# Feature-axis DFT as one pair of 64-row tiles per cycle, sequence blocks of three or four cycles, and a rounding copy moved to ScalarE

## The chip, the cores and the metric

The kernel runs on one core of one Trainium2 chip. The metric is the device time of one execution in microseconds; the time before is the median of three runs, 2136.24 us (2133.95 to 2139.14). Engines are called as the profile calls them: PE (matmul), PEld (its weight loads), DVE (vector), ACT (scalar), POOL (GpSimd), SP (sync, which issues most DMAs here).

## The reference, cut to what matters

Two branches over one sequence of 2048 rows and 640 features are mixed by a gate per row.

```
g = sigmoid((x * gate_w).sum(-1))                       # x = A_x
qkv = x @ wqkv;  32 heads of 20;  p = softmax(q k^T / sqrt(20))
a = (p v) @ wo                                          # attention
re = x @ dft_hid_re^T;  im = x @ dft_hid_im^T           # DFT over the features
b = dft_seq_re @ re - dft_seq_im @ im                   # DFT over the sequence, real part
out = g * a + (1 - g) * b
```

Both branches read the same `A_x` (`xa` in the kernel).

## The kernel before

Every matmul that must be exact in float32 is made of three matmuls in a rounded format: a value is split into a rounded part and the rest (`split`, line 90: a rounding copy by one engine, a subtraction by another), and of the four products the three large ones are summed in PSUM.

A first part (up to about 255 us) makes the projections for queries, keys and values. Then comes the main loop (line 552) of 1024 steps: 16 pairs of heads, two halves of the queries for each (32 units), 16 key tiles, two query chunks. A step makes for each of the two heads of a pair one score matmul transposed (`mixed`, L573) whose exp goes to `p` on ACT (L576), and one score matmul for the unit that follows 41 steps later (`s_mm`, L150), whose maximum DVE takes (L152). A pair of such matmuls uses the two 64-row halves of the array. All of them take their PSUM banks in turn from the five of `bank`. Every fourth step, `av_step` (L402) multiplies the last four steps' exps by the values; these 16 matmuls are called the value block here, and four steps a cycle. At the end of a unit the sums are turned into reciprocals and sent through DRAM (`unit_end`, steps 1 to 21 behind it); the negated maxima of the next unit are written into rows of the queries by four small DMAs from SP (`max_chain`). At each new pair of heads (every 64 steps, every 16 cycles) POOL issues 16 DMAs that load the stacked keys and queries (L556).

The DFTs are put between the score matmuls. First the feature axis: 64 tiles (`hid_tile`: two halves of the features, real and imaginary part, 16 row tiles), each 15 matmuls over 128 rows into one of two banks `yp` in turn, one tile in each of the three steps of a cycle that hold no value block, and one in step 0. ACT copies the bank to `raw` with a sign (L282), and SP stores it. After 64 tiles (86 steps) the input and the weights are released and the buffers of the next stage are taken (`start_dft`).

Then the sequence axis, as seven products of a Strassen scheme (`PRODUCTS`): 7 x 8 units of 16 `dft_step`s, each of three pairs of 64-row matmuls (L476), the lower half of the rows into `yp[0]`, the upper into `yp[1]`. At a unit's end ACT copies one bank (L492) and DVE adds the other (L494), later adds the result into up to two outputs (`finish_y`). `goals` says how many pairs are done by which step; half of a step's pairs stand between its two `mixed`, half behind. Every unit takes four or five cycles. The DFT matrix of the sequence comes in blocks of eight steps: at the first step of a block (s % 8 == 0) `load_c` issues the loads for the block after the next (one or two of 512 KB, into `raw` and `raw2`), at s % 8 == 4 its `finish` adds the two on POOL (L373) and splits the result into a `part` on POOL (L94, L95). Three buffers each of `raw` and `part` turn round. `run_extras` runs due DVE work in the steps with a value block, and loads and splits the other operand, `araw` to `a`, on POOL, for the next product.

At the end the attention output is projected and the three parts are added.

Of the kernel before, what the change touches and what calls it, by code (L numbers as in the profile page):

```python
# [12 lines left out]
AF = mybir.ActivationFunctionType  # L13
ALU = mybir.AluOpType
# [4 lines left out]
P = 128  # L19
# [4 lines left out]
ND = D // P  # L24
NS = S // P
NP = H // 2
HE = D // 2
# [2 lines left out]
NU = 2 * NP  # L30
BW = HE + 2
LEAD = 41
DLAG = 5

# [10 lines left out]
HT = NS // 2  # L47
UNITS = len(PRODUCTS) * HT
# [7 lines left out]
def mix_kernel(ctx: ExitStack, tc: tile.TileContext, xa, wqk, wb, cdft, wo, out):  # L56
# [33 lines left out]
    def split(dst1, dst2, src, e1, e2):  # L90
        if e1 is act:
            act.activation(dst1, src, AF.Copy)  # L92
        else:
            e1.tensor_copy(dst1, src)  # L94
        e2.tensor_tensor(dst2, src, f32(dst1), op=ALU.subtract)  # L95
# [38 lines left out]
    now, later = [-1], {}  # L134

    def at_step(i, fn):
        later.setdefault(i, []).append(fn)
# [30 lines left out]
    yp = [None, None]  # L168

    def new_y(z):  # L170
        yp[z] = ps_y.tile([P, 512], F32, name=f"yp{z}")
        return yp[z]
# [65 lines left out]
    def flush(keep=0):  # L238
        while len(stores) > keep:
            sp.dma_start(*stores.pop(0))  # L240
# [12 lines left out]
    def mm_b(j, s, ps, n):  # L253
        w = wt["b", j]
        cs = slice(s * P, (s + 1) * P)
        for d in range(ND):
            three(ps[:, :n], xs[:, 0, d, cs], xs[:, 1, d, cs], w[:, 0, d, :n], w[:, 1, d, :n], d == 0, d == ND - 1)

    def v_pair(hf, s):
# [12 lines left out]
            vst.rearrange("p a k e -> p a (k e)")))  # L272
        flush(1)

    def hid_tile(i):
        j, st = divmod(i, NS)
        hf, ri = divmod(j, 2)
        g = -1.0 if ri else 1.0
        ps = new_y(i % 2)[:, :HE]
        mm_b(2 + j, st, ps, HE)  # L280
        a = raw_tile()[:, :HE]
        act.activation(a, ps, AF.Copy, scale=g)  # L282
        stores.append((a_scr[ri, hf, st], a))
        flush(1)

    step = 0

# [72 lines left out]
    def load_c(g):  # L360
        n, j = divmod(g, 2)
        n, t = divmod(n, HT)
        raws = []
        for i, (_, th, ri) in enumerate(PRODUCTS[n][0]):
            raw = apool[0].tile([P, 1024], F32, name="raw2", bufs=2) if i and apool else raw_tile()
            o = (2 * ri + j) * 1024
            sp.dma_start(raw, cdft[th * HT + t, :, o : o + 1024])
            raws.append(raw)

        def finish():  # L370
            c = cparts[g] = part_tile()
            if len(raws) > 1:
                pool.tensor_tensor(raws[0], raws[0], raws[1], op=ALU.add if PRODUCTS[n][0][1][0] > 0 else ALU.subtract)  # L373
            split(c[:, 0], c[:, 1], raws[0], pool, pool)

        return finish

# [29 lines left out]
    def unit_end(i, n):  # L407
# [36 lines left out]
        for k, fn in ((1, store_l), (4, load_l), (10, recip), (12, store_r), (15, load_r), (19, norm), (21, store_o)):  # L444
            if n == NU - 1:
                rest.append(fn)
            else:
                at_step(i + k, fn)

    wos = {}  # L450

    seen = set()
# [2 lines left out]
    def dft_step(g):  # L455
        n, t, s = g // NS // HT, g // NS % HT, g % NS
        if s == 0:
            new_y(0), new_y(1)
            outs[n, t] = []
            for _, th, hf in PRODUCTS[n][2]:  # L460
                y = apool[0].tile([P, HE], F32, name="yt", bufs=4)
                tt = th * HT + t
                if (tt, hf) in seen:
                    sp.dma_start(y, y_scr[tt, :, hf * HE : (hf + 1) * HE])
                outs[n, t].append(y)
        if s % 8 == 0 and g // 8 + 2 < 2 * UNITS:
            cfin.append(load_c(g // 8 + 2))
        if s % 8 == 4 and cfin:
            cfin.pop()()
        c = cparts[g // 8]  # L470
        cs = slice((s % 8) * P, (s % 8 + 1) * P)
        a = at[n % 2, s]
        for z, (cz, az) in enumerate(((0, 0), (0, 1), (1, 0))):
            for h in range(2):
                r = slice(64 * h, 64 * h + 64)
                pe.matmul(yp[h][:, :HE], c[r, cz, cs], a[r, az], start=s == 0 and z == 0, stop=s == NS - 1 and z == 2)  # L476
            if z < 2:
                yield
        w = g % (HT * NS) - 16
        if n + 1 == len(PRODUCTS) and w >= 0:  # L480
            d, r = divmod(w, 8)
            if r == 0 and d < ND:
                wos[d] = raw_tile()[:, :D]
                sp.dma_start(wos[d], wo[:, d])
            if r == 5 and d < ND:
                raw = wos.pop(d)
                for h in range(2):
                    wos[d, h] = a_tile(1, 2 * d + h)
                    split(wos[d, h][:, 0], wos[d, h][:, 1], raw[:, h * HE : (h + 1) * HE], pool, pool)
        if s == NS - 1:  # L490
            m = apool[0].tile([P, HE], F32, name="m", bufs=2)
            act.activation(m, yp[0][:, :HE], AF.Copy)  # L492
            y1 = yp[1][:, :HE]
            extras.append((now[0] + 1, lambda: dve.tensor_tensor(m, y1, m, op=ALU.add)))  # L494
            for out_, y in zip(PRODUCTS[n][2], outs.pop((n, t))):
                extras.append((now[0] + 2, functools.partial(finish_y, out_, t, m, y)))
        yield
# [32 lines left out]
    def start_dft():  # L530
        flush()
        proj.release()
        apool.append(pools(name="apool", bufs=1))
    HID = 4 * NS
    ops = {}

    def load_o(tt):
# [8 lines left out]
        return finish  # L546

    total = 32 * NU
    done = hid = hid_end = 0
    goals, fins = {}, {}  # L550
    dft = itertools.chain.from_iterable(dft_step(g) for g in range(NS * UNITS))
    for i in range(total + 1):
        now[0] = i
        n, s = divmod(i, 32)
        for fn in later.pop(i, ()):
            fn()  # L556
        if s % 2 == 0:
            flush()
        if i < total:
            kt, qc = divmod(s, 2)  # L560
            if s == 0 and n % 2 == 0:
                p = n // 2
                if p + 1 < NP:
                    at_step(i + 6, functools.partial(load_v, p + 1))
                    for j, args in enumerate(load_stack(p + 1)):
                        at_step(i + 2 + j // 2, functools.partial(pool.dma_start, *args))
            q, k = q_unit(n), kst[(n // 2) % 2]
            pp = pts[n, kt, qc] = pair_tile()

            def mixed(h):  # L570
                b = 64 * h
                pt = bank()
                pe.matmul(pt, k[b : b + KROWS + 2, kt * P : (kt + 1) * P],  # L573
                          q[b : b + KROWS + 2, qc * 512 : (qc + 1) * 512], start=True, stop=True)
                most = s_mm(i + LEAD, 1 - h)
                act.activation(pp[:, h], pt, AF.Exp, scale=float(DH) ** -0.5)  # L576
                most()

            mixed(0)
            half = (done + goals.get(i, done) + 1) // 2  # L580
            while done < half:
                next(dft)
                done += 1
            mixed(1)
            s_end(i + LEAD)
        if hid_end and hid_end + 2 <= i < hid_end + 2 + HT:
            for k in range(2):
                at_step(i + 3, load_a(0, 2 * (i - hid_end - 2) + k))
        if i and i % 4 == 0:
            j = i // 2 - 2  # L590
            for kt in (j, j + 1):
                av_step(i, kt // NS, kt % NS)
            run_extras(max(done - 1, 0) // 3, 2)
        elif not hid_end:
            if hid in (NS, 2 * NS):
                flush()
                load_wb(3 + hid // NS, pool, pool)()
            hid_tile(hid)
            hid += 1
            if hid in (4 * NS - 10, 4 * NS - 6):  # L600
                flush()
                load_c((hid - 4 * NS + 10) // 4)()
            if hid == 4 * NS:
                hid_end = i + 1
                start_dft()
        else:
            if not goals:

                first = -(-(hid_end + DLAG) // 4)
                fills = [j for j in range(4 * first, total - 4) if j % 4]  # L610
                edge = [u * (len(fills) // 3) // UNITS * 3 for u in range(UNITS + 1)]
                for u in range(UNITS):
                    for f in range(edge[u], edge[u + 1]):
                        goals[fills[f]] = 3 * NS * u + 3 * NS * (f - edge[u] + 1) // (edge[u + 1] - edge[u])
            while done < goals.get(i, 0):
                next(dft)
                done += 1
        if total - 10 <= i < total - 4 and i % 2 == 0:
            tt = (i - total + 10) // 2
            fins[tt] = load_o(tt)  # L620
        if i == total - 3:
            fins[0]()
    assert done == 3 * NS * UNITS
    now[0] = total + 4
    run_extras(2 * NS * UNITS, 99)
    for i in sorted(later):
# [69 lines left out]
```

## Time and profile before

| | us |
|---|---|
| median of three runs | 2136.24 |
| the profiled execution's own time | 2140.89 |
| its span in the profile | 2139.1 |
| PE busy | 2057.7 (96%) |
| DVE busy | 1474.3 (69%) |
| ACT busy | 1249.9 (58%) |
| POOL busy | 948.7 (44%) |

In the rows of the profile, a group names its line, engine, operation, the tile written and read, the shapes and the count; after the bar stand its busy time, the mean of one in ns, and the idle time of the engine just before it with what ended most of it. A row of the timeline gives the start, the length, the engine and line, the count of merged instructions, and in brackets the idle time before it and its releaser. A row by stretches gives the stretch, its length, then busy time and count by engine; its last three columns are the granted PE clock, the mean busy share of the DMA engines and GB/s.

### The profile page before, as it was taken

The numbers are of one execution on the slowest core, as the hardware profiler recorded it, in microseconds if no ns is written. First come the engines' busy times: TensorE is split into PE (matmuls) and PEld (weight loads), VectorE is DVE, ScalarE is ACT, GpSimd is POOL, SyncE is SP. The second block draws the span as 40 slices with busy tenths as digits, with TensorE's granted clock in tenths as the row PEclk, the third lists the DMA queues.
The fourth block names the chain that finished last, engine by engine and source line by source line (L and its number), as shares of the span: only waits on it lengthen the run. The fifth ranks groups of instructions, "written<-read, shape, count | busy, mean of one in ns | idle before, by whom it ended". The sixth has DMA issues, their size and how long they took to land. (4 is left out here: it accounts for less than half of the span.)

```text
span 2139.1 us, 41869 instructions
## 1 busy us (share of the span) xinstructions
PE 2057.7 (96%) x16120; PEld 1417.3 (66%) x16120; DVE 1474.3 (69%) x2452; ACT 1249.9 (58%) x2337; POOL 948.7 (44%) x834
## 2 busy tenths in 40 slices
PE   8999999999989999999998989998999899999999
PEld 7976667676656666666565656665666566666679
DVE  3055544446878787878787878887878688888623
ACT  4221244445657676767665766666767567777761
POOL 1100000115768244435694467536644477566420
PEclk9999999999999999999999999999999999999999
DMA  7663211134464334333745374525443645353345
GB/s 227 152 179 146 105 62 45 65 107 139 132 167 136 88 99 117 96 114 126 187 136 143 126 190 145 152 89 139 128 117 110 158 146 159 118 149 113 118 138 187
DMA packets 184216, 280.86 MB, mean 131 GB/s; under 512 B 63004, under 2 KB 127548, under 8 KB 180176
## 3 DMA queue, kind: packets, MB, share of 16 engines
q1 hardware_dynamic: 158992, 246.20, 37.4%
q0 software_dynamic: 25024, 31.99, 6.9%
q8 instruction: 126, 2.06, 0.4%
q14 instruction: 74, 0.61, 0.1%
HBM read 213.81 MB, written 63.70 MB: 130 GB/s over the span
## 5 line engine op out<-in xcount | busy, mean ns | idle before, releaser
L152 DVE TENSOR_REDUCE mx<-ps 128x1 f32<-128x512 f32 x2048 | 1264.4, 682 | 395.4 <-PE ps L150 323.6
L576 ACT ACTIVATE p<-ps 128x512 f32<-128x512 f32 x2048 | 1123.1, 599 | 489.1 <-PE ps L150 414.4
L150 PE MATMUL ps<-kst,qst 60*128 60x512 f32 x2048 | 933.7, 475 | 0.7 <-ACT p L576 0.5
L573 PE MATMUL ps<-qst,kst 62*128 62x512 f32 x2048 | 813.4, 420 | 57.7 <-DVE mx L152 48.5
L476 PE MATMUL yp<-a,part 64*128 64x320 f32 x5376 | 713.9, 308 | 2.3 <-POOL part L95 1.6
L476 PEld LDWEIGHTS yp<-a,part 64*128 64x128 f32 x5376 | 605.9, 187 | 28.5 <-POOL part L95 2.3
L573 PEld LDWEIGHTS ps<-qst,kst 62*128 62x128 f32 x2048 | 372.1, 185 | 326.5 <-DVE mx L152 179.0
L402 PE MATMUL av<-p,v 128*21 128x512 f32 x4096 | 505.2, 609 | 0.1
L150 PEld LDWEIGHTS ps<-kst,qst 60*128 60x128 f32 x2048 | 363.8, 185 | 49.0 <-issue 11.6
L373 POOL TENSOR_TENSOR raw<-raw,raw 128x1024 f32<-128x1024 f32 x78 | 188.1, 2411 | 371.6 <-DMA raw<-in_cdft 241.0
L95 POOL TENSOR_TENSOR part<-raw,part 128x1024 fp32r<-128x1024 f32 x112 | 267.3, 2386 | 9.0
L402 PEld LDWEIGHTS av<-p,v 128*21 128x21 f32 x4096 | 100.2, 101 | 229.1 <-issue 222.3
L94 POOL CAST part<-raw 128x1024 fp32r<-128x1024 f32 x112 | 118.1, 1054 | 206.6 <-DMA raw<-in_cdft 166.6
L94 POOL CAST wb<-raw 128x966 fp32r<-128x966 f32 (+1 forms) x4 | 3.4, 857 | 266.7 <-DMA raw<-in_wb 266.7
L98 PE MATMUL yp<-wb,xs 128*128 128x320 f32 x320 | 106.3, 332 | 0.0
L95 POOL TENSOR_TENSOR a<-araw,a 128x320 fp32r<-128x320 f32 x112 | 97.8, 873 | 9.0
L99 PE MATMUL yp<-wb,xs 128*128 128x320 f32 x320 | 99.8, 312 | 0.0
L100 PE MATMUL yp<-wb,xs 128*128 128x320 f32 x320 | 99.7, 312 | 0.0
L92 ACT ACTIVATE p<-ps 128x512 fp32r<-128x512 f32 x40 | 23.7, 597 | 122.7 <-PE ps L100 122.7
L98 PE MATMUL ps<-xs,part 128*128 128x512 f32 x200 | 83.1, 416 | 10.0 <-ACT xs L92 6.5
L282 ACT ACTIVATE raw<-yp 128x320 f32<-128x320 f32 x64 | 28.0, 438 | 104.7 <-issue 84.4
L95 DVE TENSOR_TENSOR p<-ps,p 128x512 fp32r<-128x512 f32 x40 | 27.5, 691 | 83.3 <-ACT p L92 83.3
(70 smaller groups left out, 1541.3 us busy)
## 6 DMA issues: line engine op xcount, KB each, us to landing
raw<-in_cdft SPq DMA_DIRECT2D x192, 512.0 KB
araw<-a_scr SPq DMA_DIRECT2D x192, 160.0 KB
qk_scr<-p SPq DMA_DIRECT2D x40, 512.0 KB
y_scr<-yt SPq DMA_DIRECT2D x96, 160.0 KB
kst<-qk_scr POOLq DMA_DIRECT2D x32, 320.0 KB, 16.7
qst<-qk_scr POOLq DMA_DIRECT2D x32, 320.0 KB, 18.0
a_scr<-raw SPq DMA_DIRECT2D x64, 160.0 KB
yt<-y_scr SPq DMA_DIRECT2D x64, 160.0 KB
```

Of the source, the lines that this page charges most:

```text
L94: e1.tensor_copy(dst1, src)
L95: e2.tensor_tensor(dst2, src, f32(dst1), op=ALU.subtract)
L98: pe.matmul(ps, st1, mv1, start=first, stop=False)
L99: pe.matmul(ps, st1, mv2, start=False, stop=False)
L100: pe.matmul(ps, st2, mv1, start=False, stop=last)
L150: pe.matmul(ps, q[b : b + KROWS, qt * P : (qt + 1) * P], k[b : b + KROWS, kc * 512 : (kc + 1) * 512], start=True, stop=True)
L152: return lambda: dve.tensor_reduce(mx[n][:, h, qt, kc : kc + 1], ps, axis=AX.X, op=ALU.max)
L373: pool.tensor_tensor(raws[0], raws[0], raws[1], op=ALU.add if PRODUCTS[n][0][1][0] > 0 else ALU.subtract)
L402: pe.matmul(av[32 * j : 32 * j + DH + 1, :], v[:, kt, h * (DH + 1) : (h + 1) * (DH + 1)], pp[qc][:, h, :], start=kt == 0, stop=kt == NS - 1)
L476: pe.matmul(yp[h][:, :HE], c[r, cz, cs], a[r, az], start=s == 0 and z == 0, stop=s == NS - 1 and z == 2)
L573: pe.matmul(pt, k[b : b + KROWS + 2, kt * P : (kt + 1) * P], q[b : b + KROWS + 2, qc * 512 : (qc + 1) * 512], start=True, stop=True)
L576: act.activation(pp[:, h], pt, AF.Exp, scale=float(DH) ** -0.5)
```

## The change

The feature tiles are a generator too (`hid_tile`), written as the sequence steps are: 15 pairs of 64-row matmuls into both banks, then an ACT copy of one and a DVE addition of the other into the same `raw` tile, one step behind, and the store three steps behind. One generator, `fills`, gives feature tiles and sequence steps in turn; each of the first 64 cycles takes one feature tile, three cycles stay free for the change of buffers, and the 56 units share the rest, at three or four cycles each. Each of a cycle's six half-steps without a value block has its goal. For the blocks of the sequence matrix, `finish` now only adds the two loads (at s % 8 == 3); the split follows at s % 8 == 7, its rounding copy by ACT, its subtraction by POOL. The first two blocks are still split by POOL alone, at cycles 59 and 61, and the loads of the feature weights move to cycles 16 and 32.

```diff
@@ -30,7 +30,6 @@
 NU = 2 * NP
 BW = HE + 2
 LEAD = 41
-DLAG = 5
 
 
 
@@ -272,16 +271,27 @@
             vst.rearrange("p a k e -> p a (k e)")))
         flush(1)
 
+
     def hid_tile(i):
         j, st = divmod(i, NS)
         hf, ri = divmod(j, 2)
-        g = -1.0 if ri else 1.0
-        ps = new_y(i % 2)[:, :HE]
-        mm_b(2 + j, st, ps, HE)
+        new_y(0), new_y(1)
+        w = wt["b", 2 + j]
+        cs = slice(st * P, (st + 1) * P)
+        for d in range(ND):
+            for z, (xz, wz) in enumerate(((0, 0), (0, 1), (1, 0))):
+                for h in range(2):
+                    r = slice(64 * h, 64 * h + 64)
+                    pe.matmul(yp[h][:, :HE], xs[r, xz, d, cs], w[r, wz, d, :HE],
+                              start=d == 0 and z == 0, stop=d == ND - 1 and z == 2)
+                if (d, z) != (ND - 1, 2):
+                    yield
         a = raw_tile()[:, :HE]
-        act.activation(a, ps, AF.Copy, scale=g)
-        stores.append((a_scr[ri, hf, st], a))
-        flush(1)
+        act.activation(a, yp[0][:, :HE], AF.Copy, scale=-1.0 if ri else 1.0)
+        y1 = yp[1][:, :HE]
+        extras.append((now[0] + 1, lambda: dve.tensor_tensor(a, a, y1, op=ALU.subtract if ri else ALU.add)))
+        at_step(now[0] + 3, lambda: sp.dma_start(a_scr[ri, hf, st], a))
+        yield
 
     step = 0
 
@@ -371,7 +381,7 @@
             c = cparts[g] = part_tile()
             if len(raws) > 1:
                 pool.tensor_tensor(raws[0], raws[0], raws[1], op=ALU.add if PRODUCTS[n][0][1][0] > 0 else ALU.subtract)
-            split(c[:, 0], c[:, 1], raws[0], pool, pool)
+            return c, raws[0]
 
         return finish
 
@@ -447,6 +457,7 @@
             else:
                 at_step(i + k, fn)
 
+    HID = 4 * NS
     wos = {}
 
     seen = set()
@@ -465,8 +476,11 @@
                 outs[n, t].append(y)
         if s % 8 == 0 and g // 8 + 2 < 2 * UNITS:
             cfin.append(load_c(g // 8 + 2))
-        if s % 8 == 4 and cfin:
-            cfin.pop()()
+        if s % 8 == 3 and cfin:
+            cfin.append(cfin.pop()())
+        if s % 8 == 7 and cfin:
+            p, raw = cfin.pop()
+            split(p[:, 0], p[:, 1], raw, act, pool)
         c = cparts[g // 8]
         cs = slice((s % 8) * P, (s % 8 + 1) * P)
         a = at[n % 2, s]
@@ -531,7 +545,6 @@
         flush()
         proj.release()
         apool.append(pools(name="apool", bufs=1))
-    HID = 4 * NS
     ops = {}
 
     def load_o(tt):
@@ -546,9 +559,32 @@
         return finish
 
     total = 32 * NU
-    done = hid = hid_end = 0
+    done = 0
     goals, fins = {}, {}
-    dft = itertools.chain.from_iterable(dft_step(g) for g in range(NS * UNITS))
+    fills = itertools.chain(*(hid_tile(g) for g in range(HID)), itertools.chain.from_iterable(dft_step(g) for g in range(NS * UNITS)))
+
+
+
+    start = 4 * HID
+    HIDS = HID * 3 * ND
+    first = start // 4 + 3
+    last = total // 4 - 1
+    cycles = [(c, c + 1, 3 * ND) for c in range(HID)]
+    edge = [first + u * (last - first) // UNITS for u in range(UNITS + 1)]
+    cycles += [(edge[u], edge[u + 1], 3 * NS) for u in range(UNITS)]
+    at_goal = 0
+    for c0, c1, count in cycles:
+        slots = [(4 * c + k, z) for c in range(c0, c1) for k in (1, 2, 3) for z in range(2)]
+        for f, slot in enumerate(slots):
+            goals[slot] = at_goal + count * (f + 1) // len(slots)
+        at_goal += count
+
+    def fill(i, z):
+        nonlocal done
+        while done < goals.get((i, z), 0):
+            next(fills)
+            done += 1
+
     for i in range(total + 1):
         now[0] = i
         n, s = divmod(i, 32)
@@ -577,50 +613,34 @@
                 most()
 
             mixed(0)
-            half = (done + goals.get(i, done) + 1) // 2
-            while done < half:
-                next(dft)
-                done += 1
+            fill(i, 0)
             mixed(1)
             s_end(i + LEAD)
-        if hid_end and hid_end + 2 <= i < hid_end + 2 + HT:
+        if start + 2 <= i < start + 2 + HT:
             for k in range(2):
-                at_step(i + 3, load_a(0, 2 * (i - hid_end - 2) + k))
+                at_step(i + 3, load_a(0, 2 * (i - start - 2) + k))
         if i and i % 4 == 0:
             j = i // 2 - 2
             for kt in (j, j + 1):
                 av_step(i, kt // NS, kt % NS)
-            run_extras(max(done - 1, 0) // 3, 2)
-        elif not hid_end:
-            if hid in (NS, 2 * NS):
-                flush()
-                load_wb(3 + hid // NS, pool, pool)()
-            hid_tile(hid)
-            hid += 1
-            if hid in (4 * NS - 10, 4 * NS - 6):
-                flush()
-                load_c((hid - 4 * NS + 10) // 4)()
-            if hid == 4 * NS:
-                hid_end = i + 1
-                start_dft()
+            run_extras(max(done - HIDS, 0) // 3, 2)
         else:
-            if not goals:
-
-                first = -(-(hid_end + DLAG) // 4)
-                fills = [j for j in range(4 * first, total - 4) if j % 4]
-                edge = [u * (len(fills) // 3) // UNITS * 3 for u in range(UNITS + 1)]
-                for u in range(UNITS):
-                    for f in range(edge[u], edge[u + 1]):
-                        goals[fills[f]] = 3 * NS * u + 3 * NS * (f - edge[u] + 1) // (edge[u + 1] - edge[u])
-            while done < goals.get(i, 0):
-                next(dft)
-                done += 1
+            fill(i, 1)
+        if i % 4 == 2:
+            c = i // 4
+            if c in (NS, 2 * NS):
+                load_wb(3 + c // NS, pool, pool)()
+            if c in (HID - 5, HID - 3):
+                p, raw = load_c((c - HID + 5) // 2)()
+                split(p[:, 0], p[:, 1], raw, pool, pool)
+        if i == start:
+            start_dft()
         if total - 10 <= i < total - 4 and i % 2 == 0:
             tt = (i - total + 10) // 2
             fins[tt] = load_o(tt)
         if i == total - 3:
             fins[0]()
-    assert done == 3 * NS * UNITS
+    assert done == at_goal
     now[0] = total + 4
     run_extras(2 * NS * UNITS, 99)
     for i in sorted(later):
```

## The prediction

> **What bounds the kernel now.** I read the page first, then the steps per stretch, then one cycle in the timeline, last the waits.
>
> ```profile
> span 2139.1 us, 41869 instructions
> PE 2057.7 (96%) x16120; PEld 1417.3 (66%) x16120; DVE 1474.3 (69%) x2452; ACT 1249.9 (58%) x2337; POOL 948.7 (44%) x834
> ```
>
> PE looks full, but its ends are modelled, so I counted work per time. The main loop has 1024 steps with two score matmuls of L573 each; every fourth step a value block (L402) follows. I call four steps a cycle: eight L573 matmuls. Two answers by stretch, of L573 alone and of tile yp alone (first columns: stretch, its length, PE busy and count):
>
> ```profile
> 255.40:269.20 13.80, 3.18 (x8) 1.40 (x8) 0.88 0.18 63
> 269.20:504.70 235.50, 58.97 (x161) 23.88 (x160) 1.00 0.22 73
> 517.30:2009.30 1492.00, 715.91 (x1777) 329.40 (x1776) 0.98 0.47 134
> 1800.00:1850.70 50.70, 25.34 (x64) 11.74 (x64) 1.00 0.38 122
> ```
>
> ```profile
> 269.20:504.70 235.50, 148.90 (x900) 133.17 (x900) 0.00 (x0) 26.27 (x60) 1.00 0.22 73
> 1800.00:1850.70 50.70, 24.88 (x192) 21.69 (x192) 0.96 (x2) 0.86 (x2) 1.00 0.38 122
> ```
>
> Feature stage: 20 cycles in 235.5 us, 11.78 each, with 45 full matmuls in a cycle; the four steps before it took 13.8. Sequence stage: 222 cycles in 1492.0, mean 6.72; a quiet stretch has 8 in 50.7, 6.34 each (its usual heavy cycle included), with 24 half-height matmuls, so 12 pairs, per cycle. The stage thus holds 1492.0 - 222 x 6.34 = 84.5 us of waiting. What makes 6.3 us is in the timeline of one cycle:
>
> ```profile
> 903.10 0.50 PE L573 MATMUL ps<-qst,kst 62*128 62x512 f32 x1
> ...
> 903.67 4.96 DVE L152 TENSOR_REDUCE mx<-ps 128x1 f32<-128x512 f32 x8 [1.42 <-PE ps L150]
> ...
> 907.12 0.50 PE L150 MATMUL ps<-kst,qst 60*128 60x512 f32 x1
> ...
> 907.55 1.91 PE L402 MATMUL av<-p,v 128*21 128x512 f32 x16
> ...
> 908.55 0.48 DVE L494 TENSOR_TENSOR m<-yp,m 128x320 f32<-128x320 f32 x1
> ...
> 909.40 0.49 PE L573 MATMUL ps<-qst,kst 62*128 62x512 f32 x1
> ...
> 909.96 4.29 DVE L152 TENSOR_REDUCE mx<-ps 128x1 f32<-128x512 f32 x7 [0.93 <-PE ps L150]
> 909.99 4.58 ACT L576 ACTIVATE p<-ps 128x512 f32<-128x512 f32 x8 [1.60 <-PE ps L150]
> ```
>
> Eight score pairs run from 903.10 to 907.12, the value block from 907.55, the next cycle starts at 909.40. Eight maxima take DVE 4.96 us, eight exps ACT 4.58; both idle during the value block. Five banks serve both, so a bank comes round after five uses: the eighth score for the maxima needs the sixth exp finished. ACT starts 0.59 after a first score (909.40 to 909.99), and six exps at 0.57 end 4.01 after it; the eighth score stands at 4.02. Banks and ACT set the pace, with PE slots open between the scores. How densely PE packs:
>
> ```profile
> 1245.46 0.39 PE L573 MATMUL ps<-qst,kst 62*128 62x512 f32 x1
> 1245.69 0.46 PE L476 MATMUL yp<-a,part 64*128 64x320 f32 x4
> 1245.99 0.40 PE L573 MATMUL ps<-qst,kst 62*128 62x512 f32 x1
> ...
> 1247.42 0.52 PE L476 MATMUL yp<-a,part 64*128 64x320 f32 x4
> 1253.84 0.79 PE L573 MATMUL ps<-qst,kst 62*128 62x512 f32 x1 [5.90 <-DVE mx L152]
> ```
>
> A score pair is 0.23, two yp pairs 0.30, so 0.15 a pair. The last row is one of the long waits.
>
> **The change, part by part.**
>
> *Feature stage spread.* Its 64 tiles of 15 matmuls become 64 cycles of 15 pairs. The number of cycles stays 256, so each of the first 21 falls to sequence pace: 13.8 + 235.5 before; after, 20 x 6.34 + 4.5 (6.30 less the 1.85 of a value block that the first lacks) = 131.3. Saved: 118.0.
>
> *Denser cycles.* The sequence stage keeps 188 cycles for 56 units of 48 pairs: 36 units of three cycles (16 pairs each) and 20 of four (12, as now). A 16-pair cycle costs PE six scores with fills (0.23 + 2.67 x 0.15 = 0.63), two without, and 1.85. The two without:
>
> ```profile
> 400.50 0.50 PE L573 MATMUL ps<-qst,kst 62*128 62x512 f32 x1
> ...
> 401.17 0.41 PE L98 MATMUL yp<-wb,xs 128*128 128x320 f32 x1
> ```
>
> that is two pairs in 0.67. Sum 3.78 + 0.67 + 1.85 = 6.30, equal to the bank pace. No run shows both limits met: bounds are 0 and +0.4 (three extra pairs all behind the sixth score); I take 0.2, midway, for 103 cycles with maxima (five of 108 lie in the tail): +21 (0 to 41). With 15 pairs PE needs 0.15 less; 0.1 for 64 cycles: +6 (0 to 19).
>
> *Evacuation in two parts.* L282's copy stays; 64 DVE additions come in. The row at 908.55 is the same operation at the same place, and that cycle took 6.30, so I cost it at nothing: the value block hides it. Without that cover it is 64 x 0.48 = 31 us. The Trainium skill, TensorEngine Tiling (Array Packing), PSUM Bottleneck, warns that row tiling speeds PE but not the emptying of PSUM, which can become the limit; by it the sum would be those 31 us higher. DVE's idle 0.93 to 1.42 us per cycle speaks against it here.
>
> *ScalarE's rounding copy.*
>
> ```profile
> L373 POOL TENSOR_TENSOR raw<-raw,raw 128x1024 f32<-128x1024 f32 x78 | 188.1, 2411 | 371.6 <-DMA raw<-in_cdft 241.0 <-PE yp L476 77.4 <-PE ps L573 22.9
> L94 POOL CAST part<-raw 128x1024 fp32r<-128x1024 f32 x112 | 118.1, 1054 | 206.6 <-DMA raw<-in_cdft 166.6 <-PE yp L476 19.0 <-PE ps L178 8.8
> L92 ACT ACTIVATE xs<-raw 128x1024 fp32r<-128x1024 f32 x8 | 8.5, 1061 | 9.3 <-DMA raw<-in_xa 9.3
> ```
>
> POOL loses 110 casts of 1.05; it was not the bound, so that alone is worth nothing. ACT gains 110 copies of 1.06 in the queue that paces the scores. Where they fall: at s = 7 of each block of eight, the 22nd and 46th pair of a unit. In a three-cycle unit that is the third of a cycle's six fill slots, and the very last; in a four-cycle unit the fifth slot both times. Ahead of the sixth exp, a copy moves the eighth score by up to 1.06; the last slot falls into ACT's 1.60 of idleness and is free. Costly are 36 + 40 less those of the tail, 72; ACT's slack is nil, but a denser PE absorbs some 0.2, so 0.85: +61 (0 to 76).
>
> *What the copy waits for.* Until now only POOL waited for the matrix blocks, a whole block ahead of their use. Now exps queue behind ACT's copy, scores behind the exps' banks, and DVE behind the scores. The copy is due 21 pairs after the load's place in the program: 7.6 to 8.8 us. In quiet stretches most blocks are ready by then; not where a new pair of heads is loaded. POOL and SP rows around two of these places:
>
> ```profile
> 582.97 0.91 SPq L367 DMA_DIRECT2D raw<-in_cdft  x2
> ```
>
> ```profile
> 607.03 2.38 POOL L373 TENSOR_TENSOR raw<-raw,raw 128x1024 f32<-128x1024 f32 x1 [16.85 <-DMA raw<-in_cdft]
> 609.48 1.04 POOL L94 CAST part<-raw 128x1024 fp32r<-128x1024 f32 x1
> ```
>
> ```profile
> 1234.15 1.50 SPq L367 DMA_DIRECT2D raw<-in_cdft  x2
> ...
> 1251.73 2.33 POOL L373 TENSOR_TENSOR raw<-raw,raw 128x1024 f32<-128x1024 f32 x1 [15.91 <-DMA raw<-in_cdft]
> 1254.13 1.04 POOL L94 CAST part<-raw 128x1024 fp32r<-128x1024 f32 x1
> ```
>
> ```profile
> 582.00:606.00 24.00, 24.00 (x216) 16.20 (x216) 19.56 (x35) 16.77 (x32) 7.88 (x13) 1.00 0.95 176
> 1800.00:1850.70 50.70, 50.68 (x450) 34.31 (x449) 41.89 (x73) 36.19 (x68) 27.11 (x15) 1.00 0.38 122
> 631.70:638.60 6.90, 5.78 (x26) 2.13 (x28) 4.24 (x5) 1.87 (x4) 6.69 (x5) 0.51 0.63 202
> ```
>
> DMA is 0.95 busy there, against 0.38 in the quiet stretch (second to last column). The first block, whose place in the program PE reached 1.6 us after SP issued the load, was fit for the rounding at 609.48: about 16 us after the copy would be due. The second, reached 1.6 us before the issue, was fit at 1254.13: 13 late. These are the first and the seventh of fourteen head changes in the sequence stage; the first late block at each, read in this way, gives 116 us together (between 0.7 and 16, the doubled loads near 10, single ones near 6). Twelve of the fourteen remain there: +100. PE idle that long loses its clock: 6.9 us at 0.51 (the row above) cost 3.4; for eight such waits +27. The Trainium skill, TensorE: Matmul & The Clock Gate, Part 1, has half rate after an idle window of some 3.4 us and full rate after one busy window; one window at half would be 1.7 us, and the term +14 instead of +27; the row shows two. Away from the head changes 21 blocks with two loads would miss by 46 us in all; a wait gives the next load time, so +28. In the last feature cycles two loads share three raw buffers with the stage's copies: +5 (0 to 10).
>
> *Waits that were there.* Of the 84.5, much hung on the same crowded DMA:
>
> ```profile
> DVE lc L424 <- DMA lc<-l_scr: 32.7, 7, 6.3
> ```
>
> and, 26 steps after a head load, on rows of the maxima that SP issued late. An ACT wait ahead of them gives SP the time it lacked; I keep 15 of 84.5.
>
> Sum: -118 + 6 + 21 + 61 + 100 + 27 + 28 + 5 - 84.5 + 15 = +60.5 on a profiled time of 2140.9 (span 2139.1 and 1.8 around it), which lies 4.7 over the median of the three runs. 2136.2 + 60 = 2196; I say 2195.
>
> **Rivals.**
>
> *Faster: the loads arrive about when asked.* The waits remain as they were, scaled by twelve fourteenths (72), with 28 of small misses, and copies cost half (30): -118 + 6 + 21 + 30 + 28 + 5 - 84.5 + 72 = -40: 2096. For it: POOL, held by its subtraction behind ACT's copy, can no longer issue the head loads early in one burst; in quiet stretches loads are ready 2 to 7 us after their place. It decides from the point where a head change adds under 6 us rather than 10. Against: the bytes at a head change stay, and a block lasts 9.5 us instead of 12.6, so more loads meet there.
>
> *Much slower: SP loses its lead.* SP issues loads some 3 us ahead of PE because POOL runs ahead and frees buffers. If POOL marches with ACT, some 80 doubled blocks come 1.5 us later each, nearly all past the due point: 60.5 + 110 (with half a dozen clock losses less) = +165: 2300.
>
> *It doesn't do what it says.* If the feature pairs did not run side by side, 960 x 0.15 = 144 us return: 2340. The equal shape of L476 runs paired in every row above, so this is slight; so is DVE's addition on the path, 2226.
>
> **How the numbers follow.** Forecast 0.52, faster rival 0.33, lost lead 0.12, the last 0.03. The likeliest one's own range is 2150 to 2245. With the rivals, and copies free or full, 2085 to 2290. A measurement tells 0.2% (4 us) from nothing. Faster 0.34, with the cheapest corner of the forecast; within 0.2% 0.03; slower 0.63.
>
> **What would show it.** Right: the feature stage as 64 cycles of 6.3 to 6.5 us; quiet 16-pair cycles of 6.4 to 6.7; ACT's new row over `part` with 110 pieces of 1.06, idle before them 100 us or more, released by POOL L373 or the load; lost clock near each head change from the middle on. Wrong: ACT hardly idle before its copies (then the faster rival), 16-pair cycles at 6.3 or above 6.9, or DVE's additions waited for by PE.

## The result, and the profile after

The changed kernel takes 2194.07 us in the median of four runs (2189.79 to 2198.03), the kernel before 2137.3 beside it. The ratio is 1.0267, with a 95% interval of 1.0239 to 1.0295: slower by 57 us, where 2195 was forecast. The first lines of the page after:

```profile
span 2196.3 us, 43966 instructions
PE 2020.4 (92%) x17080; PEld 1395.5 (64%) x17080; DVE 1494.3 (68%) x2516; ACT 1348.4 (61%) x2447; POOL 830.4 (38%) x724
```

POOL gave up 118 us and ACT took 98; PE is less busy in a longer span. The score matmuls of the transposed kind alone (now L609; rows by stretches, columns as before) show both sides of the change: first the whole feature stage, then one four-cycle unit and one three-cycle unit, cycle by cycle.

```profile
261.00:682.70 421.70, 199.51 (x505) 94.03 (x504) 0.99 0.20 59
```

```profile
1832.00:1838.30 6.30, 3.16 (x8) 1.47 (x8) 1.00 0.31 102
1838.30:1845.50 7.20, 3.10 (x8) 1.47 (x8) 1.00 0.29 85
1845.50:1851.80 6.30, 3.11 (x8) 1.47 (x8) 1.00 0.22 62
1851.80:1859.00 7.20, 3.12 (x8) 1.47 (x8) 1.00 0.42 150
1859.00:1865.60 6.60, 3.10 (x8) 1.44 (x8) 1.00 0.86 271
1865.60:1872.70 7.10, 2.96 (x8) 1.34 (x8) 1.00 0.69 215
1872.70:1879.30 6.60, 3.10 (x8) 1.44 (x8) 1.00 0.00 0
```

The feature stage does 63 cycles in 421.7 us, 6.69 each; an undisturbed one takes 6.45. A cycle is called disturbed here when it is longer than its undisturbed length. In the sequence stage a cycle with 12 pairs takes 6.3 and one with 16 takes 6.6, but a cycle in which ACT makes its copy ahead of the sixth exp takes 7.2 and 7.1. The last of the seven also holds a copy, in its last slot, and pays nothing. ACT's timeline in those cycles shows both places:

```profile
1868.05 1.80 ACT L612 ACTIVATE p<-ps 128x512 f32<-128x512 f32 x3 [1.71 <-PE ps L149]
1869.75 1.05 ACT L91 ACTIVATE part<-raw 128x1024 fp32r<-128x1024 f32 x1
1870.70 1.56 ACT L612 ACTIVATE p<-ps 128x512 f32<-128x512 f32 x3
...
1878.72 1.05 ACT L91 ACTIVATE part<-raw 128x1024 fp32r<-128x1024 f32 x1
1879.67 0.43 ACT L506 ACTIVATE m<-yp 128x320 f32<-128x320 f32 x1
1879.99 0.60 ACT L612 ACTIVATE p<-ps 128x512 f32<-128x512 f32 x1
```

The first copy pushes three exps back that scores are waiting for; the second stands near the end of its cycle, where ACT would have idled 1.5 to 1.7 us. Next come the groups and the waits of the whole execution; the first row, of PE, is from the kernel before.

```profile
L150 PE MATMUL ps<-kst,qst 60*128 60x512 f32 x2048 | 933.7, 475 | 0.7 <-ACT p L576 0.5
```

```profile
L149 PE MATMUL ps<-kst,qst 60*128 60x512 f32 x2048 | 902.0, 452 | 137.3 <-ACT p L612 137.0
L91 ACT ACTIVATE part<-raw 128x1024 fp32r<-128x1024 f32 x110 | 115.8, 1052 | 109.4 <-POOL raw L383 84.2 <-DMA raw<-in_cdft 25.2
L94 POOL TENSOR_TENSOR part<-raw,part 128x1024 fp32r<-128x1024 f32 x112 | 265.8, 2373 | 463.1 <-ACT part L91 403.1 <-PE yp L490 34.6 <-issue 10.2
```

```profile
ACT part L91 <- POOL raw L383: 84.2, 17, 16.6
ACT part L91 <- DMA raw<-in_cdft: 25.2, 5, 10.7
DVE lc L434 <- DMA lc<-l_scr: 22.5, 5, 7.4
PE ps L609 <- DVE mx L151: 16.0, 8, 5.9
ACT raw L290 <- DMA a_scr<-raw: 10.7, 2, 6.6
```

ACT idles 109.4 us ahead of its 110 copies, in 22 pieces, and PE waits 137 us in all for exps; before, the same row held 0.5 us. Some 104 of the 109 us lie in the first five cycles of a pair of heads. Pieces of some 90 us end when a load of the matrix lands, directly (25.2) or through POOL's addition, which was waiting for it. The longest single piece, in the timelines of SP, POOL and ACT, with the stretch around it (all engines; the last columns are the clock, the DMA share and GB/s):

```profile
1411.91 0.81 SPq L377 DMA_DIRECT2D raw<-in_cdft  x2
```

```profile
1416.57 1.15 POOL L592 DMA_DIRECT2D qst<-qk_scr  x2
1436.18 2.33 POOL L383 TENSOR_TENSOR raw<-raw,raw 128x1024 f32<-128x1024 f32 x1 [18.46 <-DMA raw<-in_cdft]
```

```profile
1420.20 1.80 ACT L612 ACTIVATE p<-ps 128x512 f32<-128x512 f32 x3 [1.72 <-PE ps L149]
1438.55 1.06 ACT L91 ACTIVATE part<-raw 128x1024 fp32r<-128x1024 f32 x1 [16.55 <-POOL raw L383]
```

```profile
1417.80:1450.30 32.50, 15.58 (x132) 9.90 (x133) 11.16 (x20) 9.91 (x18) 11.31 (x9) 0.74 0.83 190
```

Two loads of the matrix are issued at 1412, while loads of new keys and queries are under way, and land at 1436, 24 us later; ACT, with the next exps behind the copy, stands still for 16.55 us, and PE with it. The clock falls as well. The granted clock of the whole execution, after and then before:

```profile
core 0: 2196.3 us, clock 0.965
```

```profile
core 0: 2139.1 us, clock 0.984
```

That is 0.035 x 2196 = 77 us of lost clock against 0.016 x 2139 = 34. Not all of it adds time: 30 of the 77 us and 6 of the 34 fall in pauses in which PE stands still anyway. In the longest, from 1423.2 to 1440.1, the mean granted clock is 0.64.

### The profile page after: what moved, and what is told of

Same layout as the page of the kernel before. It is cut to its first block, busy times and chain, and to the rows that moved or that the text cites. A ratio compares the mean times of both kernels' runs of the same rounds, so it can differ in the third digit from the quotient of the medians.

```text
span 2196.3 us, 43966 instructions
## 1 busy us (share of the span) xinstructions
PE 2020.4 (92%) x17080; PEld 1395.5 (64%) x17080; DVE 1494.3 (68%) x2516; ACT 1348.4 (61%) x2447; POOL 830.4 (38%) x724
## 5 line engine op out<-in xcount | busy, mean ns | idle before, releaser
L151 DVE TENSOR_REDUCE mx<-ps 128x1 f32<-128x512 f32 x2048 | 1284.8, 685 | 431.0 <-PE ps L149 396.1
L149 PE MATMUL ps<-kst,qst 60*128 60x512 f32 x2048 | 902.0, 452 | 137.3 <-ACT p L612 137.0
L609 PE MATMUL ps<-qst,kst 62*128 62x512 f32 x2048 | 801.5, 415 | 17.3 <-DVE mx L151 16.0
L490 PE MATMUL yp<-a,part 64*128 64x320 f32 x5376 | 639.1, 310 | 0.0
L490 PEld LDWEIGHTS yp<-a,part 64*128 64x128 f32 x5376 | 562.2, 189 | 23.0
L609 PEld LDWEIGHTS ps<-qst,kst 62*128 62x128 f32 x2048 | 375.3, 187 | 255.0 <-issue 71.8
L91 ACT ACTIVATE part<-raw 128x1024 fp32r<-128x1024 f32 (+1 forms) x137 | 135.6, 990 | 160.2 <-POOL raw L383 84.2
L285 PE MATMUL yp<-wb,xs 64*128 64x320 f32 x1920 | 219.7, 313 | 0.0
L285 PEld LDWEIGHTS yp<-wb,xs 64*128 64x128 f32 x1920 | 195.8, 191 | 9.5
L444 POOL TENSOR_TENSOR o<-o,rb 128x512 f32<-128x512 f32 x32 | 42.1, 1315 | 368.4 <-ACT p L612 265.0
L97 PE MATMUL ps<-xs,part 128*128 128x512 f32 x200 | 82.9, 414 | 9.8 <-ACT xs L91 6.3
L99 PE MATMUL ps<-xs,part 128*128 128x512 f32 x200 | 79.6, 398 | 1.3 <-DVE part L94 1.3
L98 PE MATMUL ps<-xs,part 128*128 128x512 f32 x200 | 79.2, 396 | 0.5 <-DVE xs L94 0.5
```

Source lines behind the costliest of these rows:

```text
L97: pe.matmul(ps, st1, mv1, start=first, stop=False)
L99: pe.matmul(ps, st2, mv1, start=False, stop=last)
L149: pe.matmul(ps, q[b : b + KROWS, qt * P : (qt + 1) * P], k[b : b + KROWS, kc * 512 : (kc + 1) * 512], start=True, stop=True)
L151: return lambda: dve.tensor_reduce(mx[n][:, h, qt, kc : kc + 1], ps, axis=AX.X, op=ALU.max)
L285: pe.matmul(yp[h][:, :HE], xs[r, xz, d, cs], w[r, wz, d, :HE], start=d == 0 and z == 0, stop=d == ND - 1 and z == 2)
L609: pe.matmul(pt, k[b : b + KROWS + 2, kt * P : (kt + 1) * P], q[b : b + KROWS + 2, qc * 512 : (qc + 1) * 512], start=True, stop=True)
```

## The experiments

Each ran beside the kernel before; ratios are to it. "After" and "the changed kernel" are the same. A diff shows the lines that matter; "..." stands for lines between.

**The copy back on POOL, all else as changed.**

```diff
-            split(p[:, 0], p[:, 1], raw, act, pool)
+            split(p[:, 0], p[:, 1], raw, pool, pool)
```

> The changed kernel with the rounding copy back on POOL (at s = 7, as its subtraction). Theory: the spread feature stage is a gain and ScalarE's copy the whole loss. The copies' own time in the exp queue goes (about 56 us: 35 units of three cycles at 0.55, 19 of four at 2 x 0.9) and ACT's waits for blocks go; of the 146 us of disturbed cycles some 66 remain, as before the change. 2194 - 56 - 80 = 2058 (2040 to 2085), faster than before. Rival 'the crowded DMA binds whoever waits for it': PE stands still there anyway, only the copies' time goes: 2138. Rival 'the spread itself is the loss': about 2190.

Measured: 2076.35 us, ratio 0.9708 (0.9659 to 0.9758). One operand in one line turns 57 us of loss into some 60 of gain. That is 118 us under the changed kernel, twice the 56 put down to the copies' own time, so both rivals fall. It is 18 over my figure, mostly because the disturbed cycles of the sequence stage hold 82 us where I had put 66.

**The copy alone, in the kernel before.** Nothing of the feature stage is changed; the first two blocks stay with POOL.

```diff
-            split(c[:, 0], c[:, 1], raws[0], pool, pool)
+            return c, raws[0]
...
-        if s % 8 == 4 and cfin:
-            cfin.pop()()
+        if s % 8 == 3 and cfin:
+            cfin.append(cfin.pop()())
+        if s % 8 == 7 and cfin:
+            p, raw = cfin.pop()
+            split(p[:, 0], p[:, 1], raw, act, pool)
```

> The kernel before with only the rounding copy moved to ScalarE (addition at s = 3, split at s = 7). Theory: nearly every copy falls ahead of the sixth exp here (units of four or five cycles), 110 x 0.9 = +99, and the waits for blocks at fourteen head changes add what they added to the changed kernel, some 70: 2137 + 170 = 2305 (2260 to 2330). Rival 'the crowded DMA binds anyway': +99 alone, 2236. Rival 'the spread is the loss': within 20 us of 2137.

Measured: 2324.32 us, ratio 1.0882 (1.0843 to 1.0921), +189 where 170 was expected. The two parts of the change do not depend on each other for their sign: the rest of the change gains with POOL's copy, and the copy loses without that rest. It loses more there. ACT idles 130.5 us ahead of its copies, against 109.4, and by their places hardly a copy falls into a free slot; the share of the places was not measured apart.

**ACT's time without its waits.**

```diff
-            split(p[:, 0], p[:, 1], raw, act, pool)
+            split(p[:, 0], p[:, 1], raw, pool, pool)
+            for _ in range(2):
+                act.activation(ddst, ddst, AF.Copy)
```

> The changed kernel with POOL making the real split, and ACT at the same places two copies of 470 columns of a constant tile onto itself, which wait for nothing: the copies' time in ACT's queue without their waits (about 1.06 us a pair). Theory: 55 us over the kernel with POOL's copy alone, 2058 + 55 = 2113. Rival 'ACT's spare time takes the copies, only waits count': equal to that kernel.

Measured: 2110.04 us, ratio 0.9875 (0.9831 to 0.9919): 34 over POOL's copy alone, not 55. The two copies together take 1.19 us, a little more than the 1.05 they stand for, and the cycles that hold them are longer by at least what was reckoned (7.3 with 16 pairs, 7.4 to 7.5 with 12). But the disturbed cycles shrink from 82 us to 58. I read this as time lost to ACT being time given to the loads.

**ACT's waits without its time.**

```diff
-            split(p[:, 0], p[:, 1], raw, act, pool)
+            act.activation(ddst, raw[:, :1], AF.Copy)
+            split(p[:, 0], p[:, 1], raw, pool, pool)
```

> The changed kernel with POOL making the real split, and ACT at the same places a copy of one column of the summed block into a scratch column: the wait without the copy's time (about 0.2 us each). Theory: 80 us of waits and lost clock over the kernel with POOL's copy alone, and 5 for the small copies, 2058 + 85 = 2143. Rival 'the crowded DMA binds anyway': within 15 us of that kernel.

Measured: 2144.95 us, ratio 1.0035 (1.0013 to 1.0058): 69 over POOL's copy alone, with 110 operations of 0.195 us. What waits, by the answer on that line:

```profile
L484 ACT ACTIVATE ddst<-raw x110: 192/195/234, 724.7 to 2033.1; 128x1 f32<-128x1 f32 x110
its engine sat idle before it (us, times) until:
  POOL raw L384: 88.0, 21
  DMA raw<-in_cdft: 18.6, 4
```

ACT idles 107 us, nearly the 109 of after, and more than half of the loss is there with hardly any work. The two halves give 34 + 69 = 103 of the 118; a long copy that also waits costs 15 more than both.

**No loads at the changes of heads.**

```diff
-                    for j, args in enumerate(load_stack(p + 1)):
+                    for j, args in enumerate(load_stack(p + 1) if p == 0 else ()):
```

> The changed kernel without the loads of stacked keys and queries after the second pair of heads (14 of 15 changes of heads; the scores of the later pairs are computed from old rows, so the output differs). Everything else, the load of the values too, stays. Theory: the copies wait because the matrix blocks share a crowded DMA with these loads; ACT's idle time before its copies falls from 109 us to under 30, and most of the 146 us of disturbed cycles goes: 2194 - 110 = 2084 (2060 to 2105). Rival 'SP and POOL have lost their lead, loads are late everywhere': idle time stays over 60, 2150 or more.

Measured: 2059.19 us, ratio 0.9629 (0.9585 to 0.9673), 135 under the changed kernel. ACT's copies are still there, but they no longer wait:

```profile
L91 ACT ACTIVATE part<-raw 128x1024 fp32r<-128x1024 f32 x110 | 115.6, 1051 | 11.9 <-POOL raw L383 11.9
```

109.4 us became 11.9. The loads at the head changes are what makes the blocks late, not a general loss of lead. The run takes out their issuing on POOL together with their bytes; that the bytes count most is read from the rows of after, where POOL's addition mostly waits for a landing. Of the 25 us beyond the expectation, some 17 are the two disturbed feature cycles and one ahead of the sequence stage, which went too.

**Full-height feature tiles, spread the same way** (on the kernel with POOL's copy: one bank in turn, `xs[:, xz, d, cs]` and `w[:, wz, d, :HE]` in one matmul, no DVE addition).

> The kernel with POOL's copy, whose feature tiles are again 15 matmuls of 128 rows into one bank in turn, without the DVE addition, but spread one per cycle as in the change. It tells what the half-height pairs are worth. If PE pays for changing between half and full height (0.2 to 0.3 us at each change in the feature stage of before), the six slots of a cycle pay some 1 us of which the bank pace hides half: feature cycles of 6.9 to 7.2 instead of 6.45, +30 to +45 on that kernel's 2076: 2112. If the change of height costs nothing, 6.45 and 2076; if the second bank and DVE's addition were what cost, 6.3 and 2066.

Measured: 2195.13 us, ratio 1.0266 (1.0215 to 1.0317): 119 over the half-height pairs, three times what I expected, and 59 over the kernel before. Two answers by stretch over 62 feature cycles, the score matmuls and the feature matmuls, and PE's timeline in part of one cycle:

```profile
276.00:804.60 528.60, 230.11 (x497) 86.48 (x496) 1.00 0.16 47
```

```profile
276.00:804.60 528.60, 235.94 (x930) 138.00 (x930) 1.00 0.16 47
```

```profile
399.69 0.50 PE L605 MATMUL ps<-qst,kst 62*128 62x512 f32 x1
399.69 0.50 PE L149 MATMUL ps<-kst,qst 60*128 60x512 f32 x1
400.12 0.70 PE L283 MATMUL yp<-wb,xs 128*128 128x320 f32 x3
400.76 0.50 PE L605 MATMUL ps<-qst,kst 62*128 62x512 f32 x1
400.76 0.49 PE L149 MATMUL ps<-kst,qst 60*128 60x512 f32 x1
401.19 0.56 PE L283 MATMUL yp<-wb,xs 128*128 128x320 f32 x2
```

528.6 / 62 is 8.5 us a cycle against 6.45. From a score pair to the first full-height matmul 0.43 us pass, where a half-height pair follows in 0.23; three full-height matmuls and the way back take 0.64, where 0.45 is the matmuls' own time at 0.15. So each change of height costs 0.2 us. Twelve in a cycle make some 2.4 us, of which the pace of the banks hides a little. The Trainium skill, TensorEngine Tiling (Array Packing), Key Properties, says that changing the tiling mode, not just the tile, drains TensorE; the trace agrees, at 0.2 us a change. The missing addition on DVE and the single bank bring no gain that shows. Spreading the stage and halving its tiles are thus one idea: the spread pays only with pairs of the scores' own height.

**Two waits of the rest taken out** (on the kernel with POOL's copy).

```diff
-            if c in (NS, 2 * NS):
+            if c in (NS + 4, 2 * NS + 4):
-        for k, fn in ((1, store_l), (4, load_l), (10, recip), (12, store_r), (15, load_r), (19, norm), (21, store_o)):
+        for k, fn in ((1, store_l), (4, load_l), (13, recip), (14, store_r), (16, load_r), (20, norm), (21, store_o)):
```

> The kernel with POOL's copy; the loads of the feature weights four cycles later (20 and 36, off the head changes), and in the chain at a unit's end DVE's reciprocal three steps later (store, load, multiplication follow by one step less each). Theory: the two feature cycles that stood 4 to 7 us for a raw buffer come down to 6.5 (-10), and the waits of DVE for its sums (41 us in 8 pieces there) mostly go, with lost clock: 2076 - 10 - 35 = 2031 (2015 to 2055). Rival: the stalls at the head changes have another last cause (the rows of the maxima), and only the 10 go: 2066.

Measured: 2048.95 us, ratio 0.9578 (0.9535 to 0.9621), the fastest of all, 27 under POOL's copy alone where 45 was expected. The feature cycles 17 and 33 came down to 6.5, which gives the 10 expected. DVE's wait for the sums fell from 40.9 us in 8 pieces to 2.3 in 2, but the whole sequence stage is only 11 us shorter, where 35 was expected, and 6 come from the cycle ahead of it. So the theory holds for the weight loads, while most of the time behind DVE's waits had another last cause, as the rival says; the cause that it names, the rows of the maxima, is not shown (PE waits 4.3 us for them). What remains in disturbed cycles, 70 us against 82, sits mostly near five head changes and has PE waiting for POOL's part in some of them:

```profile
PE yp L490 <- POOL part L93: 18.9, 4, 11.7
```

**ScalarE's copy, later and in the last slot of a cycle.**

```diff
-            split(p[:, 0], p[:, 1], raw, act, pool)
+            waiting.append((now[0], cfin.pop()))
...
+            if i % 4 == 3 and waiting and waiting[0][0] < i:
+                p, raw = waiting.pop(0)[1]
+                split(p[:, 0], p[:, 1], raw, act, pool)
```

> The changed kernel with ScalarE's copy kept, but issued at the end of a later cycle's last slot, 4 to 6 us after s = 7. Theory: there it falls in ACT's idle time under the value block (the 56 us of occupancy go), and the blocks have 12 to 14 us to arrive, so half of the waits go too: 2194 - 56 - 50 = 2088 (2070 to 2115). Rival 'ACT has no room for the copies wherever they stand': over 2150. A copy this late leaves POOL some 4 us for its subtraction before the block's use in half of the blocks; if that is short, PE waits for POOL's part and the time is above 2120.

Measured: 2192.79 us, ratio 1.0253 (1.0204 to 1.0302): nothing gained. The time is in the range of the first rival, but its cause is not there. PE and ACT in this kernel:

```profile
L489 PE MATMUL yp<-a,part 64*128 64x320 f32 x5376 | 634.4, 314 | 104.6 <-POOL part L94 104.6
L91 ACT ACTIVATE part<-raw 128x1024 fp32r<-128x1024 f32 x110 | 115.6, 1051 | 8.1 <-POOL raw L383 4.6 <-DMA raw<-in_cdft 3.5
```

ACT's waits did fall, from 109 to 8 us, and cycles with a copy in their last slot in which PE does not wait take 6.3 and 6.6, as with POOL's copy: ACT has room there. But PE now waits 104.6 us for POOL's subtraction, which can only start once ACT has copied. It is the last case of the expectation: the copy's room was taken out of the subtraction's.

**The split straight behind the addition** (on the fastest kernel).

```diff
-            cfin.append(cfin.pop()())
-        if s % 8 == 7 and cfin:
-            p, raw = cfin.pop()
+            p, raw = cfin.pop()()
             split(p[:, 0], p[:, 1], raw, pool, pool)
```

> The kernel with POOL's copy, later reciprocal and later weight loads, with the split directly behind the addition (s = 3), so that no other POOL work stands between them. Theory: what is left at the head changes is PE waiting for POOL's part (39 us in nine pieces in the last profile); a split that starts some 2 us sooner saves half of it with its lost clock: 2049 - 20 = 2029 (2010 to 2045). Rival: the landing alone decides, 2049 within 8.

Measured: 2093.27 us, ratio 0.9809 (0.9776 to 0.9841): 44 slower than the kernel it was made from, against both expectations. In its waits and SP's:

```profile
PE ps L607 <- DMA qst<-m: 29.1, 8, 9.1
PE yp L488 <- POOL part L93: 22.9, 4, 18.4
```

```profile
SPq L392 <- POOL araw L397: 146.4, 37, 10.6
```

In the kernel it was made from, SP waits 91.6 us in that row, and PE 4.3 for `qst<-m`. A reading that fits: three POOL operations in a row hold back the other operand's buffers, SP stands waiting for one of them, and the rows of the maxima queue behind it. This was not tested by itself.

## Why the prediction was right

The sign and the mechanism held. That the total came within 1 us is luck: terms were off and made up for each other. Without ACT's copies the sum has -118 + 6 + 21 + 5 = -86, and the copies with all that they cause have the other +146.5. The run with POOL's copy parts the measured +57 into -61 and +118, so the gain was put 25 too high and the loss 29 too high.

*Spread: right.* 6.44 us was forecast for a feature cycle, 6.45 came. With POOL's copy the spread, the denser cycles and the rest gain some 60 us together. Of the 25 us that are missing, some 5 are longer waits for raw buffers (below) and some 6 the cycle ahead of the sequence stage; the rest is in small pieces and stays open. That the gain hangs on the half height was not in the prediction, which priced full and half height alike at 0.15 us a matmul; the full-height run shows 2 us a cycle. The row from which it took 0.67 us for two score pairs ends at a full-height matmul, so by that run it holds one such change, 0.2.

*Denser cycles: right.* 6.54 was forecast for 16 pairs, 6.6 came, and 6.3 for 12.

*DVE's addition: right.* It costs nothing one can see: the feature cycle has the length of its pairs.

*ScalarE's copies: right in place, a little large.* +61 was forecast. Taking 0.55 for 35 three-cycle units and twice 0.9 for 19 four-cycle ones gives 53. The slot that was called free is free, and the late-copy run bears that out. What the term lacked: ACT's time alone, with other work in its place, cost only 34 net, since disturbed cycles became shorter.

*The waits: right in cause, too large in size.* ACT idles 109 us where 100 + 28 was forecast, and the kernel without the head loads shows their cause. The lost clock, put at +27, rose by 77 - 34 = 43, but outside PE's pauses, where it can cost time, only from 34 - 6 = 28 to 77 - 30 = 47, so by 19. The main loop has 19 spells of half rate against 10 before, so the eight that were counted were nearly right. The price of one, 3.4, was too high: in the trace of after half rate outlasts PE's pause by 3.2 to 6.4 us, which costs 1.6 to 3.2. By the Trainium skill, TensorE: Matmul & The Clock Gate, Part 1, full rate comes back after one busy window of some 3.4 us; the trace agrees with one to two such windows, and the +14 of the prediction, an estimate with one window a wait, came nearer than +27. The old waits, of which 15 us were kept, did not all go: DVE's wait for the sums still holds 22.5 us of 32.7, while PE's wait for the maxima fell from 48.5 to 16.0.

*Raw buffers: too small, and in another place.* +5 (0 to 10) was set for the last feature cycles; some 12 came. The waits came in cycles 17 and 33, where the loads of the feature weights fall on head changes: 10.7 us of ACT waiting for stores of `raw`, and 4.2 and 7.7 us of longer cycles. In the kernel with POOL's copy, moving those loads by four cycles took them away.

*The rivals.* The faster rival needed loads on time; it is what happens without head loads (2059). The lost lead does not occur: without head loads 11.9 us of waiting are left.

## What to carry to other kernels

Before an idle engine is given work, ask what stands behind that work in its queue and what the work waits for: 58% busy did not mean that ScalarE could wait. Leave an operation that depends on a far load on an engine whose queue nobody on the path needs, even if it is slower there, or place it where both its own inputs and its followers have slack. And when matmuls are scattered between others, give them the same tile height.

## What the runs showed of the hardware that was not expected

A change between half-height and full-height matmuls costs PE 0.2 us each way, 2 us in a cycle with twelve changes. Waits on ACT with hardly any work cost 69 us, with 110 operations of 0.195; with copies of 1.05 in their place it is 118. Work that slows PE can shorten its waits for loads, so losses do not simply add: a slowdown of 67 us worked out from the undisturbed cycles (35 x 0.7 + 19 x 2.25) cost 34. And a lower mean clock is not all lost time: 30 of 77 us fell where PE stood still anyway, and behind a pause half rate lasted 3.2 to 6.4 us more.
